# Transposing the attention weights in two half-height instructions instead of one

## The chip, the cores and the metric

The kernel runs on one core of a Trainium2 chip. The metric is the time of one launch in microseconds of device time, taken as the median of several runs; lower is better. PE is TensorE, with its weight loads shown apart as PEld; DVE is VectorE, ACT ScalarE, POOL GpSimd, SP the engine that issues the DMAs.

## The reference

Per batch and head (8 x 8 heads, 576 positions, 64 wide) two attentions are added: one over q, k and v averaged in groups of four (144 positions), repeated back to 576, and one local, in which a position sees those less than four away. The eight heads side by side are then x, the input of a mixture of four causal attentions, of which each position uses two.

```python
def _attn_ref(q, k, v):
    q_d = q.reshape(B, H, Sd, factor, D).mean(axis=3)      # k_d, v_d alike
    out_up = np.repeat(sm_attn(q_d, k_d, v_d), factor, axis=2)
    mask = np.abs(pos[:, None] - pos[None, :]) < factor
    ...
    return out_up + np.matmul(attn, v)

def _moe_ref(x, w_gate, wq, wk, wv, wo):
    logits = x @ w_gate                                     # the best 2 of 4, softmax over them: w
    for e in range(E):
        ...
        a = softmax(causal(scale * (x @ wq[e]) @ (x @ wk[e]).T))
        out += gate_e * (a @ (x @ wv[e]) @ wo[e])
```

## The kernel before

All sums are in fp32; the projections use float32r pairs (a high and a low part, three products each). The work on a batch has three stages. **Stage 1** (`s1_local`, `s1_down`, `s1_out`) goes through the four pairs of heads. Local scores are computed for ten tiles of 64 windows (`sc`), their softmax lies in `lp`; the pooled scores (`scd`) have 144 columns and lie in `dp`. In both, one head's rows lie on partitions 0 to 63 and the other's on 64 to 127. `s1_out` transposes them on TensorE (`tp`), copies them out of PSUM into `pt` and `pd`, and multiplies them with v into `o`, from which DVE builds x. **Stage 2** (`s2_q`, `s2_k`, `s2_v`, `s2_gate`) projects x; these are the dense products with 256 to 320 columns on the whole 128x128 array. **Stage 3** (`s2_scores`, `s2_trans`, `s2_av`, `s2_out`) works on two pairs of experts: scores `sq` of 64 rows of queries against all keys up to them, for two experts on the two halves of the partitions, softmax into `pr` buffers, transposes into `tq`, copies into `pta` and `ptb`, products with the values, and the output projection `po`. The stages of consecutive batches overlap: batch b is in stage 1 while b-1 is in stage 2 and b-2 in stage 3.

Products with a contraction of 64 run as 64x64 tiles, four of which lie on the array at once; in fp32 each is two hardware instructions, which is why the trace counts 40 for the 20 products of `local`.

A transpose is a TensorE instruction with the data as stationary operand and the identity as moving one. Before, it takes 128 partitions (122 or 112 where fewer are needed) by 128 columns, and one PSUM tile `tp` or `tq` holds both heads side by side. Where two blocks of rows stand the other way round on the partitions, `turned`, the identity with its halves exchanged, puts them right.

The order of the instructions is made by a planner in the kernel (`Plan`). Each operation is given its engines, an estimate of its length and its buffers; `ORDER` holds a priority for each, found ahead of time. `schedule` plays the engines forward and, on TensorE, prefers to stay in one kind of work (`MODE`, `SWX`, `SWM`) and puts in filler products on zeros (`wu`) when too little would run on the array. Copies out of PSUM may go to ACT or DVE (`"AV"`), subtractions and scalings to POOL or DVE. PSUM has two large buffers and four small ones of one bank; each transpose group before holds one small bank.

The pooling matrix `pool`, with which the first batch's v is averaged on TensorE (line 752), is built at the start by POOL: `count` writes indices, `fill_pool` turns them into a band of ones with comparisons and a product.

Of the kernel before, what the change touches and what calls it, by code (L numbers as in the profile page):

```python
# [1303 lines left out]
```

## Time and profile before

| | us |
|---|---|
| median of 3 runs | 494.53 (493.98 to 495.52) |
| the profiled execution | 495.67 |
| its span, first to last instruction | 493.9 |
| PE busy | 480.6 (97%) |
| DVE / ACT / POOL busy | 373.7 / 340.1 / 320.7 |
| mean granted clock of TensorE | 0.997 |

A row of the timeline merges equal instructions that follow each other on an engine. Its second number ends with the last one's recorded end, which for a product lies well after the next one's start, as products are pipelined. What an instruction costs the engine is therefore read from the distance between starts.

### The profile page before, as it was taken

Reading aid. Unit: us, or ns where it says so; the run is one execution under the profiler, and the core shown is the slowest. Engines: PE = TensorE matmul, PEld = TensorE weight load, DVE = VectorE, ACT = ScalarE, POOL = GpSimd, SP = SyncE. Lnnn points to the kernel's source line nnn. Section 1 sums busy time; section 2 is a strip of 40 time slices with the busy share of each in tenths; the row PEclk is TensorE's granted clock in tenths of the full one; section 3 lists DMA queues with packets and bytes.
Section 4 is the critical chain, followed back from the end, with each engine's and each line's share of the span. In section 5 each row is a group of like instructions: output and inputs, shape, how many; then the busy total and the mean of one; then the engine's idle time right before and its main releaser. Section 6 shows DMA issues by size and latency. Waiting matters only on the chain.

```text
span 493.9 us, 19034 instructions
## 1 busy us (share of the span) xinstructions
PE 480.6 (97%) x7691; PEld 431.1 (87%) x7693; DVE 373.7 (76%) x1163; ACT 340.1 (69%) x1110; POOL 320.7 (65%) x456
## 2 busy tenths in 40 slices
PE   7889999999999999999999999999999999999998
PEld 3769997999999898988999997999999887998886
DVE  8798998977868977688775888799596977342861
ACT  2697568768757758666877687757586776556773
...
PEclk9899999999999999999999999999999999999999
...
GB/s 201 242 242 108 179 157 161 121 66 69 155 100 109 184 37 119 107 159 52 71 200 75 72 115 102 148 114 109 30 237 62 45 1 3 49 32 30 49 51 97
DMA packets 43456, 52.62 MB, mean 107 GB/s; under 512 B 3304, under 2 KB 26344, under 8 KB 43368
## 3 DMA queue, kind: packets, MB, share of 16 engines
...
q8 instruction: 61, 1.00, 0.9%
...
## 4 chain that ended last, share of the span: by engine, by line
PE 79%; DVE 6%; ACT 6%; POOL 5%; DMA 3%; issue 2%; SPq 0%; POOLq 0%; DVEq 0%; ACTq 0%
PE pj L880 17%; PE po L1163 9%; PE pv L921 9%; PE sq L1025 8%; PE tq L1091 7%; PE o L1140 6%; PE o L839 4%; PE sc L694 3%; PE tp L821 3%; DMA lq<-in_qT_dram 3%; PE tp L810 3%; PE scd L767 2%; PE pv L752 2%; ACT pr L1046 1%; PE o L845 1%
## 5 line engine op out<-in xcount | busy, mean ns | idle before, releaser
L1054 POOL TENSOR_SCALAR pr<-pr,pst,gt 128x448 f32<-128x448 f32 (+8 forms) x89 | 67.0, 760 | 50.3 <-DVE pst L1051 41.4
L1046 ACT ACTIVATE pr<-pr,pst 128x320 f32<-128x320 f32 (+8 forms) x144 | 79.9, 556 | 21.6 <-DVE pst L1043 20.9
L880 PE MATMUL pj<-xh,wqk_h 128*128 128x320 f32 (+1 forms) x248 | 76.4, 308 | 0.0
L1043 DVE CUSTOM_DVE_ANT_0 pr<-sq,causal_t 128x192 f32<-128x192 f32 (+8 forms) x144 | 65.5, 483 | 11.4 <-PE sq L1025 10.8
L880 PE MATMUL pj<-xl,wqk_h 128*128 128x320 f32 (+1 forms) x248 | 72.9, 294 | 0.0
L880 PE MATMUL pj<-xh,wqk_l 128*128 128x320 f32 (+1 forms) x248 | 72.9, 294 | 0.0
L1025 PE MATMUL sq<-k,q 64*64 64x256 f32 (+6 forms) x768 | 56.1, 372 | 0.0
L1091 PE MATMUL tq<-ident,pr 128*128 128x128 f32 x368 | 51.8, 276 | 0.5 <-ACT ptb L511 0.3
L880 PEld LDWEIGHTS pj<-xh,wqk_h 128*128 128x128 f32 x248 | 46.6, 188 | 2.3 <-issue 0.8
L880 PEld LDWEIGHTS pj<-xh,wqk_l 128*128 128x128 f32 x248 | 46.7, 188 | 0.0
L880 PEld LDWEIGHTS pj<-xl,wqk_h 128*128 128x128 f32 x248 | 46.6, 188 | 0.0
L1091 PEld LDWEIGHTS tq<-ident,pr 128*128 128x128 f32 x368 | 41.0, 140 | 4.4 <-issue 1.2
L779 ACT ACTIVATE dp<-scd,dst 128x144 f32<-128x144 f32 x96 | 35.3, 379 | 13.7 <-DVE dst L774 13.1
L1152 POOL TENSOR_TENSOR ol<-oc,oh 128x256 fp32r<-128x256 f32 (+1 forms) x29 | 23.2, 803 | 32.0 <-ACT oh L1151 32.0
L715 POOL TENSOR_TENSOR lp<-lp,lst 128x640 f32<-128x640 f32 x27 | 34.6, 1280 | 13.0 <-DVE lst L714 11.3
L1025 PEld LDWEIGHTS sq<-k,q 64*64 64x64 f32 x768 | 32.5, 133 | 11.0 <-issue 1.4
L863 POOL TENSOR_TENSOR xl<-x,xh 128x576 fp32r<-128x576 f32 x25 | 35.6, 1424 | 3.9 <-ACT xh L862 3.8
L921 PE MATMUL pv<-wvg_h,xh 128*128 128x260 f32 x128 | 37.3, 292 | 0.0
L921 PE MATMUL pv<-wvg_h,xl 128*128 128x260 f32 x128 | 36.2, 283 | 0.0
L921 PE MATMUL pv<-wvg_l,xh 128*128 128x260 f32 x128 | 36.2, 283 | 0.0
L1163 PE MATMUL po<-oh,wo_h 128*128 128x256 f32 (+1 forms) x112 | 35.2, 314 | 0.0
L746 POOL TENSOR_TENSOR lr<-lr 128x512 f32<-128x512 f32 x27 | 34.7, 1285 | 0.0
...
## 6 DMA issues: line engine op xcount, KB each, us to landing
...
vx<-vg SPq DMA_DIRECT2D x8, 128.0 KB
```

The costliest lines, as they stand in the source:

```text
L715: op("l_nrm", "GV", (pool_tt(n), dve(n)), lambda e: eng[e].tensor_tensor(p(), p(), st[:, :, 2:3].to_broadcast([128, NT, W]), op=OP.mult), ...
L746: eng[e].tensor_tensor(vr[:, :, 0:2, :], vr[:, :, 0:2, :], vr[:, :, 2:4, :], op=OP.add)
L779: A.activation(p()[:, t, :], scs[t // 2]()[:, SD * (t % 2):SD * (t % 2) + SD], AF.Exp, bias=st[:, t, 4:5], scale=1.0 / 128.0, accum_out=st ...
L863: op("xl", "GV", (1360, dve(576)), lambda e: eng[e].tensor_tensor(xl(), x(), xh()[:, 0:S].bitcast(F32), op=OP.subtract), r=[x, (xh, 0)], w ...
L880: T.matmul(ps()[:, H0 + n0:H0 + n1], ww[:, c, w0 + 128 * p:w0 + 128 * p + 128], xx[b, c]()[:, n0:n1], start=(i == 0), stop=(i == 3 * NP - 1))
L921: T.matmul(ps()[:, :260], xx[b, c]()[:, 128 * t:128 * t + 128], ww[:, c, :], start=(i == 0), stop=(i == 3 * NP - 1))
L1025: T.matmul(pss[x]()[halves[e ^ (x % 2)], at + to:at + to + n1 - n0], q()[r, 64 * t:64 * t + 64], k()[r, n0:n1], start=True, stop=True)
L1043: op("s_max", "V", dve(n) + 4, lambda x=x, t=t, n=n, src=src: V.tensor_tensor_reduce(rows_of[t], src(), causal_t[:, S - 64:S + 256] if t = ...
L1046: op("s_exp", "A", 281 + n / 1.2, lambda x=x, t=t, n=n: A.activation(rows_of[t], rows_of[t], AF.Exp, bias=st[:, x, 4:5], scale=-1.0, accum ...
L1054: op("s_nrm", "GV", (327 + n / 1.2 + max(0, n - 384) * 1.1, 189 + n / 1.92), lambda g, x=x, t=t, n=n: eng[g].tensor_scalar(rows_of[t], row ...
L1091: T.transpose(ps()[:, 128 * x:128 * x + 128], block(t, j), turned if t % 2 else ident)
L1163: T.matmul(ps()[:, H1 + n0:H1 + n1], ww[:, p, 128 * c:128 * c + 128], xx[b, p]()[:, n0:n1], start=(i == 0), stop=(i == 5))
```

## The change

Every transpose becomes two instructions, one for each 64 partitions, with 64 columns of the identity, each into a PSUM bank of its own. A bank then holds one half of the partitions, for all blocks of the group, and the copies read one bank each; `pt`, `pd`, `pta` and `ptb` are laid out with the half ahead of the block. `turned` goes: the copy picks the half (`h ^ odd`). The groups of `s2_trans` become longer (up to seven blocks). The pooled scores' third tile is put on the same partitions as the others, since a transpose of one half must find one head there. The pooling matrix is built by DVE from the indices in two buffers, in two steps of three instructions. The planner's tables, estimates and the whole `ORDER` are new; `tp` and `trans` now count as the kind of work of the 64x64 products.

```diff
-XB, PTB = 1, 4
+XB, PTB = 1, 2
 ORDER = (
-    -402, -155, -134, -47, 246, 68, 331, 210, 256, -206, 122, 242, 359, 590, 448, 145, 425, 355, 456, 380, -84, 113,
...
-FR, TGT, TGT0, T0, TGT2, DW = -4.1, 3150.0, 3400.0, 228000.0, 3700.0, 12.6
+FR, TGT, TGT0, T0, TGT2, DW = -7.7, 3150.0, 3400.0, 450400.0, 3700.0, 16.5
...
-MODE = {"local": "quarter", ..., "scores": "quarter",
+MODE = {"local": "quarter", ..., "scores": "quarter", "tp": "quarter", "trans": "quarter",
...
+    def transpose(pss, z, data):
+        for x, r in enumerate(halves):
+            T.transpose(pss[x]()[:, z:z + 64], data[r, 0:128], ident[r, r])
...
 def count():
             for x, r in enumerate(halves):
-                G.iota(ck()[r, 0:640]...
+                for ck, z0, z1, k0 in ((cks[0], 0, 512, 0), (cks[1], 0, 128, 4)):
+                    G.iota(ck()[r, z0:z1]...
+        def above():
+            for x, n0, n1, own_x in ((0, 0, 512, 0), (1, 0, 128, 1), (1, 128, 192, 0)):
+                V.tensor_scalar(ges[x]()[:, n0:n1], cks[x]()[:, n0:n1], 0.0, own[:, own_x:own_x + 1], op0=OP.is_ge, op1=OP.mult)
         def fill_pool():
-            for x, n0, n1 in ((0, 0, 512), (1, 512, 640), (0, 640, 704)):
-                G.tensor_scalar(ge()[:, n0:n1], ck()[:, n0:n1], 0.0, own[:, x:x + 1], op0=OP.is_ge, op1=OP.mult)
-            G.tensor_scalar(lt(), ck(), 3.5, None, op0=OP.is_lt)
-            G.tensor_tensor(pool[:, 0:5, :]..., lt()[:, 0:640], ge()[:, 0:640], op=OP.mult)
+            for x, n0, n1 in ((0, 0, 512), (1, 512, 640)):
+                V.scalar_tensor_tensor(flat[:, n0:n1], cks[x]()[:, 0:n1 - n0], 3.5, ges[x]()[:, 0:n1 - n0], op0=OP.is_lt, op1=OP.mult)
...
-                    T.matmul(scs[t // 2]()[halves[h ^ (t // 2)], SD * (t % 2):SD * (t % 2) + SD],
+                    T.matmul(scs[t // 2]()[r, SD * (t % 2):SD * (t % 2) + SD],
...
-        for n0, n in ((0, 3), (3, 2)):
-            ps, pt = small("tp"), buf(wk, [128, n, 2, TQ], "pt", PTB)
-                for j in range(n):
-                    T.transpose(ps()[:, 128 * j:128 * j + rows], p()[0:rows, 2 * (n0 + j):2 * (n0 + j) + 2], ident[0:rows, 0:rows])
+        pss, pt = [small("tp") for _ in halves], buf(wk, [128, 2, 5, TQ], "pt", PTB)
+            for j in range(5):
+                transpose(pss, 64 * j, p()[:, 2 * j:2 * j + 2, :].rearrange("p t w -> p (t w)"))
+        for x in range(2):
+            op("tp_ev", "AV", (act(5 * TQ), dve(5 * TQ)), lambda e, x=x, pss=pss: copy(
+                e, pt()[:, x], pss[x]()[:, 0:320]...[:, :, 0:TQ]), r=[pss[x]], w=[(pt, x)])
...
-        jobs = {..., 3: [[(6, 0), (6, 1), (6, 2)], [(5, 0), (5, 1), (5, 2)]],
-                4: [[(8, 0), (8, 1), (8, 2)], [(8, 3), (8, "d")], [(7, 0), (7, 1), (7, 2), (7, 3)]]}[u]
+        jobs = {..., 3: [[(6, 0), (6, 1), (6, 2), (5, 0), (5, 1), (5, 2)]],
+                4: [[(8, 0), (8, 1), (8, 2), (8, 3), (8, "d")], [(7, 0), (7, 1), (7, 2), (7, 3)]]}[u]
...
-                    T.transpose(ps()[:, 128 * x:128 * x + 128], block(t, j), turned if t % 2 else ident)
+                    transpose(pss, 64 * x, block(t, j))
...
+            for h in range(2):
+                op("t_ev", "AV", (act(k) + m, dve(k) + m), lambda e, h=h, ev=ev: ev(e, h), r=[pss[h]],
```

Two places in the order on the engines. The first is TensorE at batch 0's first products of stage 3. `pr_131`, `pr_130` and the like are the softmax rows of one block of queries, `tq` and `tp` the transposes, `o` the products with v or with the values. Before:

```order
L880 MATMUL pj<-xl,wqk_h 128x256
L1091 MATMUL tq<-ident_121,pr_128 128x128 x2
L1091 MATMUL tq<-ident_121,pr_133 128x128 x2
L810 MATMUL tp<-ident_121,lp 128x122 x3
L1091 MATMUL tq<-ident_121,pr_131 128x128 x3
L1091 MATMUL tq<-ident_121,pr_130 128x128 x4
L1091 MATMUL tq<-ident_121,pr_133 128x128 x4
L1091 MATMUL tq<-ident_121,pr_129 128x128 x3
L1091 MATMUL tq<-ident_121,pr_131 128x128 x2
L810 MATMUL tp<-ident_121,lp 128x122 x2
```

and now:

```order
L879 MATMUL pj<-xl,wqk_h 128x256
L556 MATMUL tq<-ident,pr_130 128x64 x8
L838 MATMUL o_2198<-pt,lv 64x58 x12
L556 MATMUL tq<-ident,pr_131 128x64 x10
L838 MATMUL o_2198<-pt,lv 64x58 x4
L838 MATMUL o_2198<-pt,lv 64x56 x4
L1137 MATMUL o_2235<-pta,vg 64x192 x2
```

Four blocks of 128 columns have become eight instructions of 64, and the transposes that stood together in one run are strewn between 64x64 products: over the whole program TensorE goes from transposes to 64x64 products 79 times where it went 44 times, and back 64 times where it went 30 times; between dense and 64x64 products it goes 86 times (65 before), between dense products and transposes 88 times (79 before). It has 49 fillers where it had 37.

The second is the start, on POOL. `ck` are the indices, `dh`, `qd` and `kd` the averaged q and k, `lr` rings of rows of v. Before:

```order
L591 IOTA ck 64x640
L593 IOTA ck 64x64
L734 TENSOR_TENSOR dh<-lq 128x288
L735 TENSOR_TENSOR qd<-dh 128x144
L619 MEMSET lr_98 128x512
L614 MEMSET pool 128x256
L619 MEMSET lr_99 128x512
L598 TENSOR_SCALAR ge<-ck,own 128x512
L598 TENSOR_SCALAR ge<-ck,own 128x128
L598 TENSOR_SCALAR ge<-ck,own 128x64
L599 TENSOR_SCALAR lt<-ck 128x704
L600 TENSOR_TENSOR pool<-lt,ge 128x640
```

and now on DVE, where `lp` are the first local scores with their mask:

```order
L610 MEMSET causal_t 128x256
L611 MEMSET causal_t 128x128
L612 TENSOR_SCALAR causal_t<-nrow 128x64
...
L600 TENSOR_SCALAR ge<-ck,own 128x512
L600 TENSOR_SCALAR ge<-ck,own 128x128
L600 TENSOR_SCALAR ge<-ck,own 128x64
L703 SCALAR_TENSOR_TENSOR lp<-sc,lmask 128x640
L706 TENSOR_REDUCE lst_72<-lp 128x10
L605 SCALAR_TENSOR_TENSOR pool<-ck,ge 128x512
L605 SCALAR_TENSOR_TENSOR pool<-ck,ge 128x128
L607 SCALAR_TENSOR_TENSOR pool<-ck,ge 128x2x32
```

The five large passes have left POOL; on DVE there are six smaller ones, behind the masks and around the first local scores.

## Rows read from the trace of the kernel before

**Rows 1.** The page of the kernel before: busy time of each engine with its share of the span and its instructions, and the granted clock of TensorE in tenths of full speed in 40 equal slices of the span.

```profile
PE 480.6 (97%) x7691; PEld 431.1 (87%) x7693; DVE 373.7 (76%) x1163; ACT 340.1 (69%) x1110; POOL 320.7 (65%) x456
...
PEclk9899999999999999999999999999999999999999
```

**Rows 2.** The page: the chain of work that ended last, by engine.

```profile
PE 79%; DVE 6%; ACT 6%; POOL 5%; DMA 3%; issue 2%; SPq 0%; POOLq 0%; DVEq 0%; ACTq 0%
```

**Rows 3.** Groups of PE's instructions by line and shape: out<-in, shape, count | busy us, mean ns of one as recorded | idle before.

```profile
L1091 PE MATMUL tq<-ident,pr 128*128 128x128 f32 x368 | 51.8, 276 | 0.5 <-ACT ptb L511 0.3
...
L810 PE MATMUL tp<-ident,lp 122*128 122x122 f32 x160 | 24.8, 272 | 0.9 <-DVE lp L715 0.3 <-DVE pst L1043 0.3 <-ACT pt L511 0.2
...
L821 PE MATMUL tp<-ident,dp 112*128 112x112 f32 x96 | 19.4, 260 | 0.0
L821 PE MATMUL tp<-ident,dp 128*128 128x128 f32 x64 | 18.2, 290 | 3.2 <-ACT dp L788 0.8 <-ACT pta L511 0.7 <-ACT ptb L511 0.5
```

**Rows 4.** PE's timeline around 156 us, instructions that follow each other merged: start us, us from the first start to the last end, what, count.

```profile
155.82 0.28 PE L880 MATMUL pj<-xh,wqk_l 128*128 128x256 f32 x1
155.94 0.28 PE L880 MATMUL pj<-xl,wqk_h 128*128 128x256 f32 x1
156.06 0.93 PE L1091 MATMUL tq<-ident,pr 128*128 128x128 f32 x7
156.82 0.37 PE L821 MATMUL tp<-ident,dp 128*128 128x128 f32 x2
157.12 0.57 PE L839 MATMUL o<-pt,lv 64*64 64x58 f32 x24
157.52 0.55 PE L1025 MATMUL sq<-k,q 64*64 64x192 f32 x9
```

**Rows 5.** PE's timeline from 161 to 164 us, the same columns.

```profile
161.01 0.81 PE L694 MATMUL sc<-lk,lq 64*64 64x64 f32 x40
161.64 0.72 PE L1025 MATMUL sq<-k,q 64*64 64x64 f32 x12
162.29 0.74 PE L810 MATMUL tp<-ident,lp 122*128 122x122 f32 x5
162.96 0.81 PE L694 MATMUL sc<-lk,lq 64*64 64x64 f32 x40
163.70 0.41 PE L880 MATMUL pj<-xh,wqk_h 128*128 128x320 f32 x1
```

**Rows 6.** The timeline from 6 to 14 us, all engines, the rows that make or wait for the pooling matrix and one two-input pass of DVE; in brackets idle time before, and what ended it.

```profile
6.24 3.20 POOL L598 TENSOR_SCALAR ge<-ck,own 128x512 f32<-128x512 int32 x3
...
8.04 0.81 DVE L697 SCALAR_TENSOR_TENSOR lp<-sc,lmask 128x640 f32<-128x640 f32 x1
...
9.40 1.98 POOL L599 TENSOR_SCALAR lt<-ck 128x704 f32<-128x704 int32 x1
...
11.46 1.53 POOL L600 TENSOR_TENSOR pool<-lt,ge 128x640 f32<-128x640 f32 x1
...
13.05 1.30 PE L752 MATMUL pv<-lv,pool 128*128 128x128 f32 x7 [2.48 <-POOL pool L600]
```

**Rows 7.** Stretches of 25 us: length, then busy us (and instructions) of PE, PEld, DVE, ACT and POOL, the granted clock, DMA share and GB/s.

```profile
25.00:50.00 25.00, 23.01 (x458) 19.92 (x458) 22.37 (x63) 21.41 (x76) 21.61 (x22) 1.00 0.64 172
50.00:75.00 25.00, 24.47 (x454) 23.06 (x453) 22.63 (x64) 15.76 (x56) 21.89 (x27) 1.00 0.54 163
75.00:100.00 25.00, 23.82 (x422) 21.63 (x425) 22.27 (x64) 19.99 (x66) 22.77 (x30) 1.00 0.50 140
```

**Rows 8.** Weight loads in the timeline, from 171.9 and from 157.0 us: start us, us from the first start to the last end, what, count.

```profile
172.10 0.20 PEld L821 LDWEIGHTS tp<-ident,dp 128*128 128x128 f32 x2 [0.53 <-DVE oc L1149]
...
157.12 0.31 PEld L839 LDWEIGHTS o<-pt,lv 64*64 64x64 f32 x14 [0.16 <-issue]
```

**Rows 9.** Groups of weight loads (PEld) by line and shape, columns as in rows 3.

```profile
L839 PEld LDWEIGHTS o<-pt,lv 64*64 64x64 f32 x1280 | 28.4, 134 | 4.8 <-issue 2.7 <-DVE pst L1051 0.2 <-ACT pta L511 0.2
...
L821 PEld LDWEIGHTS tp<-ident,dp 128*128 128x128 f32 x64 | 8.9, 140 | 5.8 <-ACT pta L511 1.2 <-ACT dp L788 0.9 <-ACT ptb L511 0.8
```

**Rows 10.** PE's timeline from 176 to 177.2 us.

```profile
176.01 0.57 PE L839 MATMUL o<-pt,lv 64*64 64x58 f32 x24
176.51 0.66 PE L1091 MATMUL tq<-ident,pr 128*128 128x128 f32 x4
177.00 0.38 PE L810 MATMUL tp<-ident,lp 122*128 122x122 f32 x2
```

**Rows 11.** PE's timeline from 41.9 us, at the pooled scores.

```profile
41.92 0.56 PE L767 MATMUL scd<-kd,qd 64*64 64x144 f32 x10
42.27 0.34 PE L845 MATMUL o<-pd,vd 64*64 64x144 f32 x2
```

**Rows 12.** Groups of DVE's instructions by line and shape, columns as in rows 3.

```profile
L513 DVE COPY ptb<-tq 128x384 f32<-128x384 f32 x21 | 11.5, 552 | 15.5 <-PE tq L1091 15.5
...
L513 DVE COPY pd<-tp 128x192 f32<-128x192 f32 x17 | 5.9, 351 | 3.8 <-PE tp L821 3.6
```

**Rows 13.** Two stretches, 25 to 100 us and the rest, for the instructions that write or read tq alone, then for those of tp: length, then busy us (and instructions) of PE, PEld, DVE and ACT, the granted clock, DMA share and GB/s.

```profile
25.00:100.00 75.00, 3.13 (x23) 2.52 (x23) 0.98 (x2) 2.68 (x7) 1.00 0.56 159
...
25.00:100.00 75.00, 13.01 (x87) 9.38 (x85) 7.50 (x18) 6.50 (x18) 1.00 0.56 159
```

More of the change, by code (lines that the diff above doesn't have):

```diff
@@ L436 @@
 TICK = 10240 / 3
-MODE = {"local": "quarter", "down": "quarter", "o1": "quarter", "o1d": "quarter", "av": "quarter", "scores": "quarter",
+MODE = {"local": "quarter", "down": "quarter", "o1": "quarter", "o1d": "quarter", "av": "quarter", "scores": "quarter", "tp": "quarter", "trans": "quarter",
         "q": "dense", "k": "dense", "v": "dense", "wo": "dense"}
@@ L441 @@
        ("column", "quarter"): 100.0, ("quarter", None): 165.0, ("quarter", "dense"): 170.0, ("quarter", "column"): 150.0}
-LAG = {"scores": 85.0, "down": 60.0, "local": 50.0, "o1d": 20.0}
-SWM = {None: 1.3, "quarter": 1.1, "column": 1.8, "dense": 1.6}
+LAG = {"scores": 85.0, "down": 60.0, "local": 50.0, "o1d": 20.0, "tp": 40.0, "trans": 40.0}
+SWM = {None: 5.1, "quarter": 1.6, "column": 4.1, "dense": 4.9}
 SWB, MARG = 0, 2.0
-LOCK = {"V": {"vd", "xl", "l_sub", "l_nrm", "d_nrm", "xt", "wlo", "s_nrm", "o_lo"},
+LOCK = {"V": {"vd", "xl", "l_sub", "l_nrm", "d_nrm", "xt", "wlo", "s_nrm", "o_lo", "c_ge", "c_pool"},
         "G": {"vd", "kd", "qd", "l_sub", "l_nrm", "d_nrm", "xl", "xt", "wlo", "o_lo", "g_rank", "g_mask", "g_nrm"}}
-RATE = {"local": 2.1, "down": 1.2, "tp": 1.18, "trans": 1.18, "o1": 2.1, "o1d": 2.2, "av": 2.0, "scores": 2.1}
+RATE = {"local": 2.1, "down": 1.2, "tp": 2.1, "trans": 2.1, "o1": 2.1, "o1d": 2.2, "av": 2.0, "scores": 2.1}
 F32R_COL, F32R_MM = 0.4167, 13.2
+QT = 15.8
 def dense(n, cols):
@@ L604, in masks @@
+            z = [t()[:, 128:192].rearrange("p (k m) -> p k m", m=2 * WT) for t in (cks[1], ges[1])]
+            V.scalar_tensor_tensor(pool[:, 5:7, 64 - WT:64 + WT], z[0], 3.5, z[1], op0=OP.is_lt, op1=OP.mult)
         def masks():
@@ L614, in constants @@
         op("c_zero", "G", 320, lambda: G.memset(pool[:, 5:7, :], 0.0), w=[(PL, 1)])
-        op("c_cnt", "G", 1800, count, w=[ck], alloc=[ck])
-        op("c_pool", "G", 4100, fill_pool, r=[ck], w=[ge, lt, (PL, 1)], alloc=[ge, lt])
+        op("c_cnt", "G", 2100, count, w=cks, alloc=cks)
+        op("c_ge", "V", 560, above, r=cks, w=ges, alloc=ges)
+        op("c_pool", "V", 930, fill_pool, r=cks + ges, w=[(PL, 1)])
         plan.unit = ("constants", 1)
@@ L620, in constants @@
         plan.unit = ("constants", 2)
-        op("c_mask", "V", 650, masks, w=[CT])
-        op("c_rank", "V", 260, ranks, w=[ML])
+        op("c_mask", "V", 1370, masks, w=[CT])
+        op("c_rank", "V", 180, ranks, w=[ML])
     wqk_h = cst.tile([128, NP, 512], F32R, name="wqk_h")
@@ L815, in s1_out @@
-        pss, pd = [small("tp") for _ in range(2)], buf(wk, [128, 5, 2, NQD], "pd", NPD)
-        def trd(x):
-            flat, kr = dp().rearrange("p t w -> p (t w)"), 64 + NQD
-            jobs = (((2 * SD + WT, 208, 128), (SD + WT, 112, kr), (0, 0, kr)), ((2 * SD - 48, 112, 128), (SD - 64, 0, kr)))[x]
-            for at, z, n in jobs:
-                T.transpose(pss[x]()[:, z:z + n], flat[0:n, at:at + 128], turned if n == 128 else ident[0:n, 0:n])
-        def evd(e, x):
-            n = (3, 2)[x]
-            copy(e, pd()[:, 3 * x:3 * x + n], strided(pss[x]()[:, 0:NQD], (112 + 16 * x, n), (64, 2)))
@@ new lines, in s1_out, with trd @@
+        op("tp", "T", 20 * QT, tr, r=[p], w=pss, alloc=pss + [pt])
+        for x in range(2):
+            op("tp_ev", "AV", (act(5 * TQ), dve(5 * TQ)), lambda e, x=x, pss=pss: copy(
+                e, pt()[:, x], pss[x]()[:, 0:320].rearrange("p (j q) -> p j q", q=64)[:, :, 0:TQ]), r=[pss[x]], w=[(pt, x)])
+        pss, pd = [small("tp") for _ in halves], buf(wk, [128, 2, 5, NQD], "pd", NPD)
+        def trd(pss=pss):
+            flat = dp().rearrange("p t w -> p (t w)")
+            for i, at in enumerate((0, SD + WT, 2 * SD + WT, SD - 64, 2 * SD - 48)):
+                transpose(pss, 80 * i - 16 * (i in (2, 4)), flat[:, at:at + 128])
@@ L829, in s1_out @@
+        op("tp", "T", 20 * QT, trd, r=[dp], w=pss, alloc=pss + [pd])
+        for x in range(2):
+            op("tp_ev", "AV", (act(5 * NQD), dve(5 * NQD)), lambda e, x=x, pss=pss: copy(
+                e, pd()[:, x], pss[x]()[:, 0:400].rearrange("p (j q) -> p j q", q=80)[:, :, 0:NQD]), r=[pss[x]], w=[(pd, x)])
         o, up = big("o1"), buf(wk, [128, SD], "up")
@@ L831, in s1_out, with av @@
         xl = XL[b, c] = buf(wk, [128, S], "xl", 8, F32R)
-        def av(k0, pt):
-            for t in range(k0, k0 + pt.shape[1]):
+        def av(k0, k1):
+            for t in range(k0, k1):
                 z, n = TQ * t, min(TQ, SH - TQ * t)
@@ L1005, in s2_gate @@
         op("g_nrm", "G", 200, norm, r=[WR, gst], w=[cmt])
[L1006 removed]
+        op("g_out", "A", 1020, spread, r=[cmt], w=[gt], alloc=[gt])
     PT = {}
@@ L1081, in s2_trans @@
         for js in jobs:
-            ps, first = small("tq"), []
+            pss, first = [small("tq") for _ in halves], []
             parts = sorted(set(place(*x)[0] for x in js))
@@ L1099, in s2_trans @@
                 part, jj, q0 = place(t, j)
-                if runs and runs[-1][0] == part and runs[-1][4] != 2 and jj == runs[-1][2] + runs[-1][1] and q0 == runs[-1][3]:
-                    runs[-1][1] += 1
-                    runs[-1][4] = 1
-                elif runs and runs[-1][0] == part and runs[-1][4] != 1 and jj == runs[-1][2] and q0 == runs[-1][3] + 64 * runs[-1][1]:
-                    runs[-1][1] += 1
-                    runs[-1][4] = 2
-                else:
-                    runs.append([part, 1, jj, q0, 0, x])
@@ L1109, in ev @@
-            def ev(eng, runs=runs, ps=ps):
-                for part, n, jj, q0, way, x in runs:
-                    pt, src = PT[b, p, part], ps()[:, 128 * x:128 * (x + n)]
+                last = runs[-1] if runs else None
+                if last and last[0] == part and last[6] == t % 2 and last[4] != 2 and jj == last[2] + last[1] and q0 == last[3]:
+                    last[1] += 1
+                    last[4] = 1
+                elif last and last[0] == part and last[6] == t % 2 and last[4] != 1 and jj == last[2] and q0 == last[3] + 128 * last[1]:
+                    last[1] += 1
+                    last[4] = 2
+                else:
+                    runs.append([part, 1, jj, q0, 0, x, t % 2])
@@ L1112, in ev @@
+            def ev(eng, h, runs=runs, pss=pss):
+                for part, n, jj, q0, way, x, odd in runs:
+                    pt, src = PT[b, p, part], pss[h]()[:, 64 * x:64 * (x + n)].rearrange("p (j q) -> p j q", q=64)
                     if way == 2:
-                        copy(eng, pt()[:, jj, :, q0:q0 + 64 * n].rearrange("p e (t q) -> p t e q", q=64),
-                             src.rearrange("p (t e q) -> p t e q", e=2, q=64))
-                    else:
-                        copy(eng, pt()[:, jj:jj + n, :, q0:q0 + 64], src.rearrange("p (j e q) -> p j e q", e=2, q=64))
@@ L1117, in s2_trans @@
-            k, m = 128 * len(js), 60 * (len(runs) - 1)
-            op("t_ev", "AV", (act(k) + m, dve(k) + m), ev, r=[ps],
-               w=[(PT[b, p, x[0]], (x[0], x[2], x[3])) for x in runs])
+                        copy(eng, pt()[:, h ^ odd, jj, q0:q0 + 128 * n].rearrange("p (t q) -> p t q", q=128)[:, :, 0:64], src)
+                    else:
+                        copy(eng, pt()[:, h ^ odd, jj:jj + n, q0:q0 + 64], src)
+            k, m = 64 * len(js), 60 * (len(runs) - 1)
+            for h in range(2):
+                op("t_ev", "AV", (act(k) + m, dve(k) + m), lambda e, h=h, ev=ev: ev(e, h), r=[pss[h]],
+                   w=[(PT[b, p, x[0]], (x[0], x[2], x[3], h ^ x[6])) for x in runs])
@@ L1140, in mm @@
                         T.matmul(obs[x]()[r, q0:q1], vg()[kr, j, 64 * (2 * p + e):64 * (2 * p + e) + 64],
-                                 pt()[kr, j, e, q0:q1], start=j == 0, stop=j == len(jobs) - 1 and part == 0 and x == 1)
+                                 pt()[kr, e, j, q0:q1], start=j == 0, stop=j == len(jobs) - 1 and part == 0 and x == 1)
             for x, jj, q0, to, vv, at in tails:
@@ L1144, in mm @@
                     T.matmul(obs[x]()[r, to:to + 64], vv()[halves[x], at, 64 * (2 * p + e):64 * (2 * p + e) + 64],
-                             pt()[halves[x], jj, e, q0:q0 + 64], start=to < z, stop=(x, at) != (1, 1))
+                             pt()[halves[x], e, jj, q0:q0 + 64], start=to < z, stop=(x, at) != (1, 1))
         cost = 15 + 1.667 * (sum(q1 - q0 for _, q0, q1 in jobs) + 64 * (len(tails) + 1) // 2) + 8 * (len(jobs) + 1)
```

63 lines of the change are left out of this document (23 added, 40 removed), and 278 rows, old and new, of the table ORDER.

## The prediction

> **What bounds the kernel now.** I read the page first. PE is busy 97% of the span, DVE 76%, ACT 69%, POOL 65%, and the granted clock stands at nine tenths or more of full speed (2.4 GHz) in every slice but the second [rows 1]. The chain that ended last is PE for 79% of the span [rows 2]. Because a busy PE is not a PE at its peak, I then went to the timeline and priced PE by the distance between starts, not by the recorded duration. Seven transposes of 128 columns reach from 156.06 to 156.82, 0.109 us each, though one is recorded with 0.276 us [rows 3, 4]. Five of 122 columns take 0.67 with a head and a tail that I price below, so 0.104 each [rows 5]. Priced so, dense products, 64x64 products, transposes, the pooling product and the fillers add up to some 433 us of the 494: PE is the bound nearly throughout, and a microsecond of PE work saved is close to a microsecond of time. The exceptions are the start, where PE sits idle 2.48 us for the pooling matrix [rows 6], and the stage from 25 to 100 us, where DVE is busy 22.4, 22.6 and 22.3 us of each 25 [rows 7].
>
> **The transposes.** Removed: 368 of 128 columns (0.109 each, 40.1 us), 160 of 122 (0.104, 16.6), and 64 of 128 and 96 of 112 columns on line 821 (7.0, and at 0.095 in proportion to the columns 9.1): 72.8 us of PE [rows 3 to 5]. Added: 2 x 688 instructions of 64 partitions and 64 columns. No row shows such a pair. The nearest is a round of four 64x64 instructions on the same array: 40 of them take 0.63 [rows 5], less the first uncovered load of 0.057 that is 0.0144 each, 0.058 for a round of four with 64 columns. The 58-column ones give the same (24 in 0.40) [rows 4], so the round is set by its loads as much as by its columns. A new pair moves 64 columns in each half, as a round does, and loads two blocks of 64x128, as many weights as a round's four blocks of 64x64. So I take 0.058. From below it is 64 columns at the old pace, 0.0545. From above it is two loads one behind the other: a load of 128 columns keeps the next one off for 0.06 (two take 0.20, one lasts 0.140) [rows 8, 9], 0.114 for the pair. Sum: 688 x 0.058 = 39.9, **a gain of 32.9 us**, with bounds of 35.3 gained and 5.6 lost.
>
> **Changes of tile shape.** From dense products to 128x128 transposes nothing is lost: 155.94 to 156.06 is the pace of the dense ones. From transposes into 64x64 work it costs 0.094 (156.82 to 157.12 is 0.30, of which the two transposes are 0.206) [rows 4]. Out of 64x64 work it costs 0.11 for the drain (40 take 0.74 before a dense product, 0.63 before more 64x64 work; 24 take 0.50 before a transpose, 0.40 otherwise) and 0.056 for the first load that nothing covers [rows 4, 5, 10], 0.166 together. In the order of both programs I count the borders. Before: 70 into 64x64 work, 69 out of it, 18.0 us. After, if the new 64x128 instructions mix freely with 64x64 ones, as the 64x64 ones mix among themselves: 88 in and 86 out, 22.6 us, **4.5 lost**. If they drain against 64x64 work as well, 79 more into it and 64 more out of it: 40.6 us, 22.6 lost. If they mix with the dense ones instead, 11.5 lost; if with both, 6.6 won. No row decides, since the kernel before has no 64x128 instruction. I take the first, because what mixes with 64x64 work in the trace also uses the halves of the rows apart; both ends stay in the range. The Trainium skill speaks against this (TensorEngine Tiling, Key Properties): it says that a change of tiling mode, other than a change of tile, drains the engine, and it lists 64x128 and 64x64 as different configurations. The trace has the drain, 0.11 us, but only between 128x128 and 64x64. By that rule it is the second of the four sums above.
>
> **The scores of the pooled stage (line 767).** The third pair of products now writes the same two quarters of the array as the first two. Before, the third's passes ran beside them: ten passes take 0.35 [rows 11], 0.035 each where two quarters alone would give 0.06. At worst two passes of 0.12 come on top in each of 32 units, 7.7 us; at best the next 64x64 work fills the free quarters. I take **2 us lost**, nearer to the best because 64x64 work follows at once in these rows.
>
> **The copies out of PSUM.** The same columns leave PSUM in more and smaller copies: DVE gets 193 where it had 112, ACT 219 where it had 160. A DVE copy of 384 columns takes 0.552, one of 192 0.351 [rows 12]: about 0.15 fixed and 1.05 ns per column. Worked out over the forms, DVE gets some 18 us more. With the other work that the new order shifts to and from DVE (three more poolings of each kind, four fewer subtractions) DVE goes from 374 to about 392 us, 83% of a span of 474. Between 25 and 100 us, where 110 of the 688 transposes stand [rows 13], a sixth, it would reach 70.6 us of 75, so that this stage can hardly shrink: 5 of its 5.8 us are not won. Elsewhere DVE goes from 73% to about 82%; its answers come later, and the new order has twelve more fillers, all of them in its first sixth, which marks where PE has to be kept busy; I put 4 us on that. **9 us lost**, from 2 to 16. What hides the copies now is the PE work between a transpose and its user; were that cover gone, PE would wait for a copy of 0.35 to 0.45 per group. Each group now takes two of the four small PSUM banks, at nothing, since the groups per pair of heads fall from seven or eight to five.
>
> **The pooling matrix.** The large passes on POOL reach from 6.24 to 12.99 us [rows 6]. DVE has no such rows; its nearest is 0.81 for 640 columns, so two passes over 704 columns are about 1.8, behind the index counting that stays on POOL. PE's idle time of 2.48 goes, except what DVE's own queue (the masks and the first local scores stand ahead) takes back: **2 us gained**, from 0 to 2.5. Table entries alone move instructions, and cost nothing by themselves.
>
> **Sum.** -32.9 + 4.5 + 2 + 9 - 2 = -19.4. The profiled execution took 495.67 us, a span of 493.9 and 1.8 around it; that gives 476.3. It lies 1.1 above the median of the runs, so the forecast is 475.
>
> **The rivals.**
> 1. The new transposes drain against 64x64 work. For it: every border between shapes that the trace has costs 0.1 to 0.17. Against it: they share the halves of rows. 18 us more, of which the waits give back 4, since a slower PE waits less: 489.
> 2. They mix with dense work and not with 64x64 work: 7 more at the borders, 482. For it: both use all 128 columns of the array. Against it: one uses whole rows, the other halves.
> 3. The loads of the two halves do not overlap, and the change ends **slower**: 0.114 a pair, 688 x 0.114 = 78.4 for 72.8, 5.6 lost where 32.9 were to be gained. With the borders (4.5), the pooled scores (2), waits of 2 on a PE that is slower, and the start (-2) it is 12 on top: 507. It decides from about 0.086 a pair, where the gain is used up. Against it: fourteen 64-column loads go in 0.31 [rows 8], a round of four in 0.06 where each is recorded with 0.134 [rows 9], so loads into different parts do overlap. By the Trainium skill (TensorE: Matmul & The Clock Gate, LDWEIGHTS) a load takes its columns over 1.2 per ns, whatever the rows, so 107 ns for 128 columns, and a pair could not be shorter than that. The trace disagrees: the second load of 128 columns began 0.06 after the first [rows 8].
> 4. The new transposes drain against nothing and DVE follows: 6.6 gained at the borders in place of 4.5 lost, waits of 4: 459. DVE's share in the stage from 25 to 100 us speaks against it [rows 7].
> 5. It does not do what it says: the halves overlap in part (0.08 to 0.09 a pair), and the extra borders take the rest: 493 to 496.
>
> **Chances.** The forecast 0.54 (467 to 482); rival 1 0.17 (483 to 492.5); rival 2 0.09; rival 3 0.10; rival 4 0.05; rival 5 0.05. A measurement of this kernel tells 0.3%, 1.5 us, from no change. Faster: 0.54 + 0.17 + 0.09 + 0.05, less 0.01 for the slow end of rival 1: 0.84. Same: 0.05. Slower: 0.11. The range runs from 463 to 492, which leaves out rivals 3 and 5 and most of 4.
>
> **What would show it.** In the profile after, eight new transposes in a row should take 0.23 to 0.25 us from the first start to the next group's; 0.45 is rival 3. A row of 64x64 work ahead of a transpose should take no longer than ahead of more 64x64 work; 0.11 longer is rival 1. The lines of the pooling matrix should leave POOL, and the first pooling product start near 11 us. DVE should be busy near 390 us. A granted clock under full speed anywhere after the start would make all of it wrong, since every price here was read at full speed.

## The result, and the profile after

The kernel after takes 501.33 us (median of 4 runs, 500.68 to 502.54) where the kernel before, on the same chip, took 495.02 (4 runs, 493.98 to 495.68). The ratio is 1.0132, with a 95% interval of 1.0104 to 1.0161: slower by 1.3%, where 475 had been forecast. The profiled execution took 501.08 us, 5.4 more than the one of before, with a span of 499.3.

The page of the kernel after: busy time, the granted clock, the chain by engine [rows 1, 2].

```profile
PE 487.9 (98%) x8391; PEld 423.7 (85%) x8393; DVE 392.2 (79%) x1256; ACT 334.8 (67%) x1150; POOL 314.7 (63%) x451
...
PEclk9989999999999999999999999999999999999999
...
PE 83%; DVE 10%; ACT 3%; DMA 2%; issue 1%; POOL 1%; SPq 0%; DVEq 0%; ACTq 0%; POOLq 0%
```

PE bounds it more than before, at the same clock. DVE's 392.2 us are the 392 of the prediction. So the loss must be looked for on PE. The groups of PE by shape [rows 3]:

```profile
L556 PE MATMUL tq<-ident,pr 64*128 64x64 f32 x736 | 38.5, 232 | 2.1 <-ACT oh L1148 0.7 <-DVE oc L1146 0.5 <-DVE ptb L511 0.4
...
L556 PE MATMUL tp<-ident,dp 64*128 64x64 f32 x320 | 17.5, 232 | 1.2 <-DVE vd L511 0.8 <-ACT dp L794 0.2 <-DVE pt L511 0.2
L556 PE MATMUL tp<-ident,lp 64*128 64x64 f32 x320 | 16.8, 231 | 0.3 <-DVE pst L1042 0.3
```

The recorded busy time fell from 114 us to 73, and says nothing of the price. PE's timeline from 294.6 us, where all four kinds of border stand within 2 us, does [rows 4, 5]:

```profile
294.52 0.28 PE L929 MATMUL pv<-wvg_h,xh 128*128 128x260 f32 x1
294.63 0.28 PE L929 MATMUL pv<-wvg_l,xh 128*128 128x260 f32 x1
294.84 0.52 PE L556 MATMUL tp<-ident,lp 64*128 64x64 f32 x10
295.30 0.81 PE L700 MATMUL sc<-lk,lq 64*64 64x64 f32 x40
296.04 0.53 PE L556 MATMUL tp<-ident,dp 64*128 64x64 f32 x10
296.49 0.38 PE L1160 MATMUL po<-oh,wo_h 128*128 128x256 f32 x1
```

Read it by starts. Dense products follow each other by 0.12, but the first transpose comes 0.21 after the last of them: for 0.09 PE starts nothing. This is the drain, and there is none in [rows 4]. Ten half transposes, five pairs, take 0.46 and 0.45. The trace has a pair every 0.061 within a run, so five are 0.31; 0.05 goes for the first pair's load, which nothing covers (the second pair starts 0.112 after the first), and 0.10 for a drain at the end, towards 64x64 work and dense work alike. The 40 products of the local scores take 0.74 ahead of transposes, where they took 0.63 ahead of other 64x64 work [rows 5]: 0.11 again. Drain and first load together are some 0.15 for each border. **The 64x128 instructions drain against both other shapes, on both sides.** The whole trace has it so, not these two microseconds alone: the last pair of a run stands 0.156 us from what follows, ahead of 64x64 work (76 runs) as ahead of dense work (38), where another pair would stand at 0.062 (medians without waits, worked out from the starts). Behind it the second dense product comes 0.225 after the first, where 0.12 is their pace, so the border into dense work costs some 0.20; out of the old transposes it cost 0.03.

For the whole kernel I added up, by the tile written, the time from each matmul's start to the next one's, its slot (worked out from the traces; waits and drains lie with the instruction ahead of them; the last three columns are experiments below):

| us | before | after | third_other | more_borders | quarter_products |
|---|---|---|---|---|---|
| transposes (tq, tp) | 83.9 | 67.2 | 68.5 | 115.8 | 111.0 |
| dense (pj, pv, po) | 218.7 | 225.4 | 226.3 | 225.5 | 225.5 |
| pooled scores (scd) | 15.1 | 26.2 | 20.0 | 25.8 | 26.2 |
| o, sq, sc | 151.8 | 155.8 | 155.4 | 155.3 | 159.7 |
| fillers, pooling product | 22.1 | 22.1 | 22.2 | 24.0 | 22.2 |
| sum | 491.4 | 496.7 | 492.3 | 546.3 | 544.6 |

(The 115.8 contain the added one-column products, 144 x 0.204 = 29.4. Such sums agree with the spans within rounding and the two ends.) The change won 16.7 us on the transposes' own slots, not 32.9, and gave back 6.7 on dense work, 4.0 on 64x64 work and 11.1 on the pooled scores.

The copies on DVE, the largest groups [rows 12], and the stage that the prediction took for the tightest [rows 7]:

```profile
L511 DVE COPY pt<-tp 128x290 f32<-128x290 f32 x35 | 15.1, 451 | 4.9 <-PE tp L556 4.8
L511 DVE COPY ptb<-tq 128x192 f32<-128x192 f32 x38 | 11.8, 351 | 7.0 <-PE tq L556 6.9
```

```profile
25.00:50.00 25.00, 22.80 (x422) 19.52 (x421) 23.48 (x64) 19.86 (x67) 21.68 (x21) 0.93 0.66 193
50.00:75.00 25.00, 25.00 (x481) 22.94 (x480) 18.67 (x55) 17.25 (x58) 20.84 (x25) 1.00 0.46 123
75.00:100.00 25.00, 24.43 (x468) 20.90 (x468) 23.43 (x74) 20.66 (x79) 22.84 (x33) 1.00 0.49 140
```

DVE has 65.6 us here, not the 70.6 that were worked out, and PE 72.2. The start, DVE's and PE's timeline [rows 6]:

```profile
8.46 1.96 DVE L605 SCALAR_TENSOR_TENSOR pool<-ck,ge 128x512 f32<-128x512 int32 x2
```

```profile
10.05 1.83 PE L758 MATMUL pv<-lv,pool 128*128 128x128 f32 x14
12.36 0.81 PE L700 MATMUL sc<-lk,lq 64*64 64x64 f32 x40 [0.49 <-DMA lq<-in_qT_dram]
```

The matrix left POOL, and the first pooling product starts at 10.05 without a wait, where it started at 13.05 after 2.48 of idle time.

### The profile page after: what moved, and what is told of

It is laid out like the page before. It is cut to its first block, busy times and chain, and to the rows that moved or that the text cites. A ratio compares the mean times of both kernels' runs of the same rounds, so it can differ in the third digit from the quotient of the medians.

```text
span 499.3 us, 20630 instructions
## 1 busy us (share of the span) xinstructions
PE 487.9 (98%) x8391; PEld 423.7 (85%) x8393; DVE 392.2 (79%) x1256; ACT 334.8 (67%) x1150; POOL 314.7 (63%) x451
## 4 chain that ended last, share of the span: by engine, by line
PE 83%; DVE 10%; ACT 3%; DMA 2%; issue 1%; POOL 1%; SPq 0%; DVEq 0%; ACTq 0%; POOLq 0%
PE pj L879 21%; PE po L1160 9%; PE pv L920 9%; PE sq L1024 8%; PE o L1137 6%; PE tq L556 6%; PE tp L556 5%; PE o L838 4%; PE scd L773 4%; PE sc L700 3%; PE o L844 2%; PE pv L929 1%; DVE pr L1042 1%; PE po L1184 1%; DMA wst<-in_wo_dram 1%
## 5 line engine op out<-in xcount | busy, mean ns | idle before, releaser
L1045 ACT ACTIVATE pr<-pr,pst 128x192 f32<-128x192 f32 (+8 forms) x144 | 80.0, 558 | 26.6 <-DVE pst L1042 24.6
L1053 POOL TENSOR_SCALAR pr<-pr,pst,gt 128x192 f32<-128x192 f32 (+8 forms) x88 | 58.7, 671 | 56.7 <-DVE pst L1050 39.6
L879 PE MATMUL pj<-xh,wqk_h 128*128 128x320 f32 (+1 forms) x248 | 77.8, 314 | 0.0
L1024 PE MATMUL sq<-k,q 64*64 64x256 f32 (+6 forms) x768 | 57.3, 374 | 0.2 <-DVE x L856 0.2
L862 POOL TENSOR_TENSOR xl<-x,xh 128x576 fp32r<-128x576 f32 x29 | 41.3, 1426 | 9.2 <-ACT xh L861 9.2
L785 ACT ACTIVATE dp<-scd,dst 128x144 f32<-128x144 f32 x96 | 35.2, 374 | 10.8 <-DVE dst L780 10.3
L556 PE MATMUL tq<-ident,pr 64*128 64x64 f32 x736 | 38.5, 232 | 2.1 <-ACT oh L1148 0.7
L511 DVE COPY ptb<-tq 128x192 f32<-128x192 f32 (+4 forms) x95 | 29.7, 348 | 12.6 <-PE tq L556 12.2
L556 PEld LDWEIGHTS tq<-ident,pr 64*128 64x128 f32 x736 | 29.1, 138 | 11.6 <-issue 3.5
L752 POOL TENSOR_TENSOR lr<-lr 128x512 f32<-128x512 f32 x28 | 36.3, 1296 | 0.0
```

What stands on the lines that cost most here:

```text
L556: T.transpose(pss[x]()[:, z:z + 64], data[r, 0:128], ident[r, r])
L752: eng[e].tensor_tensor(vr[:, :, 0:2, :], vr[:, :, 0:2, :], vr[:, :, 2:4, :], op=OP.add)
L785: A.activation(p()[:, t, :], scs[t // 2]()[:, SD * (t % 2):SD * (t % 2) + SD], AF.Exp, bias=st[:, t, 4:5], scale=1.0 / 128.0, accum_out=st ...
L862: op("xl", "GV", (1360, dve(576)), lambda e: eng[e].tensor_tensor(xl(), x(), xh()[:, 0:S].bitcast(F32), op=OP.subtract), r=[x, (xh, 0)], w ...
L879: T.matmul(ps()[:, H0 + n0:H0 + n1], ww[:, c, w0 + 128 * p:w0 + 128 * p + 128], xx[b, c]()[:, n0:n1], start=(i == 0), stop=(i == 3 * NP - 1))
L1024: T.matmul(pss[x]()[halves[e ^ (x % 2)], at + to:at + to + n1 - n0], q()[r, 64 * t:64 * t + 64], k()[r, n0:n1], start=True, stop=True)
```

## The experiments

Three explanations are tested. Theory A: the drains of the new shape took what the transposes won. Theory B: the third pair of pooled scores, now behind the first two, costs several times the 2 us of the prediction. Theory C, the rival: PE's work did shrink, and more copies on DVE took it back.

**third_other** (after):

```diff
-                    T.matmul(scs[t // 2]()[r, SD * (t % 2):SD * (t % 2) + SD],
+                    T.matmul(scs[t // 2]()[halves[h ^ (t // 2)], SD * (t % 2):SD * (t % 2) + SD],
```

> The kernel after, with only the third pair of products of the pooled scores put back on the two quarters of the array that the first two pairs leave free (the third tile then holds the two heads' rows the other way round, and what reads it is not changed, so the outputs of the pooled part mix two heads). Theory B, that the third pair now runs behind the first two instead of beside them: the slots of this line fall from 26.2 us to about 15, the time from 501.3 to 490 to 493. The prediction's own size of this term (2 us): 499. Theory A (borders between tile shapes) and theory C (DVE is late) say nothing of it, and by C alone, PE not being the bound, the time would stay within 1 us.

Measured: 495.60 us, ratio to before 0.9999 (0.9979 to 1.0019), 6 us less than after.

**before_third_same** (before):

```diff
-                    T.matmul(scs[t // 2]()[halves[h ^ (t // 2)], SD * (t % 2):SD * (t % 2) + SD],
+                    T.matmul(scs[t // 2]()[r, SD * (t % 2):SD * (t % 2) + SD],
```

> The kernel before, with only the third pair of products of the pooled scores put on the same two quarters as the first two (the third tile's heads change places, as in the other run, and what reads it is not changed). Theory B: 8 to 11 us slower, 503 to 506 beside 495. The prediction's size: 497. If the free quarters are filled by the next 64x64 work: under 1 us.

Measured: 500.96 us, ratio 1.0120 (1.0083 to 1.0157), 5.4 us more. Both ways the line costs 5 to 6.5 us: nearly three times the prediction's 2, less than the 8 to 11 I expected of theory B. The groups of PE by shape in after, third_other, before and before_third_same, in this order:

```profile
L773 PE MATMUL scd<-kd,qd 64*64 64x144 f32 x384 | 31.1, 290 | 0.0
```

```profile
L773 PE MATMUL scd<-kd,qd 64*64 64x144 f32 x384 | 22.7, 294 | 0.0
```

```profile
L767 PE MATMUL scd<-kd,qd 64*64 64x144 f32 x384 | 22.4, 294 | 0.5 <-DVE kd L732 0.5
```

```profile
L767 PE MATMUL scd<-kd,qd 64*64 64x144 f32 x384 | 30.6, 288 | 0.4 <-DVE kd L732 0.4
```

The mean of one doesn't move (288 to 294 ns); what moves is how much of it lies beside another. The timelines of after and of third_other at the same work:

```profile
60.44 0.82 PE L773 MATMUL scd<-kd,qd 64*64 64x144 f32 x9
60.99 0.26 PE L838 MATMUL o<-pt,lv 64*64 64x58 f32 x1
```

```profile
60.86 0.58 PE L773 MATMUL scd<-kd,qd 64*64 64x144 f32 x10
61.18 0.30 PE L838 MATMUL o<-pt,lv 64*64 64x58 f32 x4
```

The next 64x64 work starts 0.55 after the first pooled product in the one and 0.32 in the other: it doesn't fill the free quarters. 32 units by 0.23 are 7.4; the rest of the 11.1 us that the slots of scd gained is the new order's. That it is held up because it stands behind the third pair in PE's queue is argued from the order, not shown: in third_other four passes start within 0.03 us, where after has two and then none for 0.17. So the third pair starts there ahead of the second, and PE does let some work pass.

**less_dve** (after):

```diff
-  ... V.tensor_reduce(st[:, :, 0], p(), op=OP.add, axis=AX.X) ...
+  ... V.tensor_reduce(st[:, :, 0], p()[:, :, 0:32], op=OP.add, axis=AX.X) ...
...
-  V.tensor_reduce(dst()[:, 0:n], s4, op=OP.add, axis=AX.X)
+  V.tensor_reduce(dst()[:, 0:n], s4[:, :, 0:2], op=OP.add, axis=AX.X)
```

> The kernel after, with less work on DVE and nothing else changed: the sums of the local probabilities read 32 of the 64 columns of each tile, and DVE's poolings of q and k read two of the four columns (both leave out half of a sum, so the numbers differ). DVE's busy time falls by some 22 us, from 392 to about 370, below what it was in the kernel before (374). Theory A and B, that the loss is PE work: 0 to 3 us faster, 498 to 501. Theory C, that the more and smaller copies on DVE hold PE up: 10 us or more faster, 491 or less.

Measured: 500.27 us, ratio 1.0095 (1.0069 to 1.0121), 1 to 2 us less than after. The page:

```profile
PE 487.9 (98%) x8393; PEld 424.0 (85%) x8393; DVE 372.3 (75%) x1256; ACT 334.4 (67%) x1150; POOL 314.8 (63%) x451
```

20 us less on DVE, and PE's busy time to the tenth the same. Nor did PE wait more than before: span less busy time is 11.4 us in after, 13.3 in before. Theory C falls.

**more_borders** (after), once in each group of transposes:

```diff
...
+  T.matmul(pss[0]()[lo, 511:512], ident[lo, 0:64], ident[lo, 0:1], start=True, stop=True)
```

> The kernel after, with a 64x64 product of one column added in the middle of each of the 144 groups of half transposes, on the lower half's quarter and into a column of PSUM that nobody reads. Theory A, that 64x128 transposes and 64x64 products drain against each other on both sides: 0.136 + 0.166 = 0.30 us for each group, 43 us in all, of which waits may give back some: 530 to 545. The prediction's assumption that the two mix freely: two passes of 0.015 to 0.03 each, 4 to 9 us, 505 to 510. Theory C: less than 5 us, since PE would have slack.

Measured: 549.82 us, ratio 1.1110 (1.1072 to 1.1148), 48.5 us more than after: 0.337 for each of the 144, a little over the 0.30 of theory A, with nothing given back. Counted without idle time and at full clock, PE's work grew by 46.9 us, 0.33 each. PE's timeline at the work that was shown of after:

```profile
321.82 0.28 PE L937 MATMUL pv<-wvg_l,xh 128*128 128x260 f32 x1
322.03 0.34 PE L560 MATMUL tp<-ident,lp 64*128 64x64 f32 x4
322.30 0.27 PE L555 MATMUL tp<-ident 64*64 64x1 f32 x2
322.50 0.40 PE L560 MATMUL tp<-ident,lp 64*128 64x64 f32 x6
322.83 0.81 PE L704 MATMUL sc<-lk,lq 64*64 64x64 f32 x40
```

The two passes of one column keep the next transpose off for 0.20, and the five pairs reach over 0.80 in place of 0.46.

**quarter_products** (after):

```diff
-  T.transpose(pss[x]()[:, z:z + 64], data[r, 0:128], ident[r, r])
+  for c, rc in enumerate(halves):
+      T.matmul(pss[x]()[rc, z:z + 64], data[r, 64 * c:64 * c + 64], ident[r, r], start=True, stop=True)
```

> The kernel after, in the same order, with each half transpose replaced by two 64x64 products with the identity, so that this work has the tile shape of the other 64x64 work. Each block is then 8 passes of 64 columns in place of 2: two rounds of four at 0.058 us, 0.117 for 0.061, 38 us more. Theory A: the 143 borders between transposes and 64x64 work vanish with it, 79 x 0.136 + 64 x 0.166 = 21 us, so 517 to 520. If these borders cost nothing: 538 to 541.

Measured: 547.11 us, ratio 1.1006 (1.0966 to 1.1046), above both. The timeline and the waits of PE:

```profile
321.13 0.28 PE L930 MATMUL pv<-wvg_l,xh 128*128 128x260 f32 x1
321.34 0.81 PE L557 MATMUL tp<-ident,lp 64*64 64x64 f32 x40
321.97 0.76 PE L701 MATMUL sc<-lk,lq 64*64 64x64 f32 x40
322.55 0.94 PE L557 MATMUL tp<-ident,dp 64*64 64x64 f32 x40
323.43 0.39 PE L1161 MATMUL po<-oh,wo_h 128*128 128x256 f32 x1
```

```profile
PE tq L557 <- issue: 7.7, 6, 1.9
PE tp L557 <- issue: 5.3, 5, 2.3
PE o L839 <- issue: 3.0, 2, 2.1
PE o L1142 <- issue: 3.0, 3, 1.2
PE sq L1025 <- issue: 1.4, 1, 1.4
```

The borders did vanish: the 40 products of the local scores take 0.58, not 0.74, and the first five blocks 0.63, 0.17 more than in after, where the passes alone add 0.28. The whole trace says the same by its medians: five blocks of `tp` between dense products take 0.741 where they took 0.456 in after, all of the 0.28; ahead of 64x64 work, 0.631 for 0.456; between 64x64 work, 0.588 for 0.456. (The second five blocks of this row, 0.88, are slower than the others of their kind, 0.80; they hold pauses of up to 0.05.)

But PE sits idle 20.4 us in these five rows, 22.8 in all 20 waits of this kind, put down to "issue" (in after all such waits are 1.0 us). Without them it would be some 524, nearer to theory A's 517 to 520 than to 538. The queue that loads instructions, after and then quarter_products, tells what they are:

```profile
q8 instruction: 66, 1.08, 0.9%
```

```profile
q8 instruction: 98, 1.61, 1.3%
```

Its packets have 16 KB, and there is one for every 254 to 256 products and weight loads of PE in both kernels: it is PE's own program. Counted in PE's records, the 20 waits lie whole multiples of 256 apart, to within one, and each ends 1.2 to 1.8 us after a packet has landed (worked out from the trace). So PE waited for instructions. Why these packets came too late and others didn't is open, so the run supports theory A by its rows more than by its time.

**third_fixed** (after): third_other with the third tile's heads put right.

```diff
...
-  for i, at in enumerate((0, SD + WT, 2 * SD + WT, SD - 64, 2 * SD - 48)):
+  for i, at in enumerate((SD - 64, 0, SD + WT, 2 * SD + WT, 2 * SD - 48)):
...
-  e, pd()[:, x], pss[x]()[:, 0:400].rearrange("p (j q) -> p j q", q=80)[:, :, 0:NQD]) ...
+  e, pd()[:, x ^ z, a:n], pss[x]()[:, 80 * a:80 * n].rearrange("p (j q) -> p j q", q=80)[:, :, 0:NQD])
+  for z, a, n in ((0, 0, 3), (1, 3, 5)) ...
...
```

> The kernel after with the third pair of the pooled scores on the other two quarters, as in the first of these runs, and the third tile's heads now put right in the copies out of PSUM: its blocks stand last in each bank and are copied to the other half's place, two copies for one (64 copies more over ACT and DVE, some 0.15 us each). Theory B by the runs so far (5.5 us for this line): 495 to 497. If the additional copies held PE up: 499 or more, but less work on DVE brought 1.1 us only, so they should cost under 1.

Measured: 498.05 us, ratio 1.0044 (1.0009 to 1.0080): 3 to 4.5 us less than after, and still no faster than before. That is above the 495 to 497 expected. After and the profiled execution of this kernel (499.45) each have one wait of PE, at local scores some 24 us into the span, for which the profile names nothing ("issue"):

```profile
PE sc L700 <- issue: 0.8, 1, 0.8
```

```profile
PE sc L700 <- issue: 3.3, 1, 3.3
```

They stand at the same place, the 704th and the 706th of PE's records, and are of the kind that quarter_products explains: in this execution a late load of instructions accounts for 2.5 us.

**fewer_borders** and **far_fewer_borders** (third_fixed, the planner's table; 24.0 for 6.0 in the second):

```diff
...
-  "tp": "quarter", "trans": "quarter"
+  "tp": "row", "trans": "row"
...
+  ("dense", "row"): 146.0, ("row", "dense"): 151.0, ("quarter", "row"): 150.0, ("row", "quarter"): 140.0
...
-  SWM = {None: 5.1, "quarter": 1.6, "column": 4.1, "dense": 4.9}
+  SWM = {None: 5.1, "quarter": 6.0, "row": 6.0, "dense": 6.0}
-  FR, TGT, TGT0, T0, TGT2, DW = -7.7, 3150.0, 3400.0, 450400.0, 3700.0, 16.5
+  FR, TGT, TGT0, T0, TGT2, DW = -7.7, 2100.0, 2100.0, 450400.0, 3700.0, 16.5
...
```

> The kernel of third_fixed, with the planner told that the half transposes are a kind of their own that drains against both others (0.14 to 0.17 us at each change of kind, where it had put them with the 64x64 products), a patience of 6 for all kinds, and a lower mark for fillers. The order that comes out has 290 changes of kind where after has 337 (tr and 64x64: 98 for 143), and 42 fillers for 49. Theory A: 47 borders at 0.15 and 7 fillers at 0.43, 7 + 3 us less than third_fixed: 485 to 489, if the new order makes no new waits; a table of due times that was made for another order speaks for some, so up to 495. If the borders cost nothing: 493 to 496, from the fillers alone.

> As fewer_borders with a patience of 24: 258 changes of kind, 58 fillers. Theory A: 79 borders at 0.15 less, 11.8 us, 9 fillers more, 3.9 us: 486 to 490, plus the waits that a patience of 24 makes, which may take all of it back (up to 500).

Measured: 532.47 us (1.0739, 1.0680 to 1.0797) and 549.62 (1.1078, 1.1016 to 1.1141). Both miss, by 35 us and more. The page of fewer_borders:

```profile
PE 497.8 (94%) x8386; PEld 422.9 (80%) x8386; DVE 381.9 (72%) x1269; ACT 345.4 (65%) x1210; POOL 315.6 (59%) x453
...
PE   6987998999999899999799998999899999999998
...
PEclk9699999999999988999879997999999999999999
```

PE is idle 32.9 of 530.7 us, against 14.2 of 497.7 in third_fixed, and the clock is granted at 0.965 on the mean, against 0.993: the slices at 0.7 or 0.8 of full speed (15th, 16th, 20th, 21st and 25th; a part of each at 1.2 GHz, the rest at 2.4) hold idle time of PE or stand behind a slice that does (the 14th, 20th and 25th, one to three tenths idle). Others as idle, the 4th, 7th and 29th, keep full speed. 18.7 us of idle time and some 15 of clock are all of the 33 by which the spans differ, and leave nothing for the 7 us of the 47 borders. Both terms are too rough to rule these 7 out, and the last pair of a run stands 0.156 from what follows here too. These two runs tell that an order is worth more than the borders in it; they say nothing for theory A.

**matrix_on_pool** (after); the comparison in `above` goes to POOL in the same way:

```diff
-  V.scalar_tensor_tensor(flat[:, n0:n1], cks[x]()[:, 0:n1 - n0], 3.5, ges[x]()[:, 0:n1 - n0], op0=OP.is_lt, op1=OP.mult)
+  G.tensor_scalar(lt, cks[x]()[:, 0:n1 - n0], 3.5, None, op0=OP.is_lt)
+  G.tensor_tensor(flat[:, n0:n1], lt, ges[x]()[:, 0:n1 - n0], op=OP.mult)
...
```

> The kernel after, with the pooling matrix built by POOL instead of DVE, in the same order. The prediction's price of this part is 2 us (0 to 2.5); the two traces show the third local scores begin at 12.36 us in after and at 15.78 in before. So 2 to 3.5 us slower than after, 503 to 505; if DVE's queue or the first stage takes it back anyway, within 1 us of 501.3.

Measured: 505.55 us, ratio 1.0192 (1.0140 to 1.0244), 3 to 4 us more than after. PE's timeline has the wait back:

```profile
13.74 2.57 PE L762 MATMUL pv<-lv,pool 128*128 128x128 f32 x12 [3.75 <-POOL pool L607]
```

**before_matrix_dve** (before), the version that the others point to:

```diff
-  G.tensor_scalar(ge()[:, n0:n1], ck()[:, n0:n1], 0.0, own[:, x:x + 1], op0=OP.is_ge, op1=OP.mult)
+  V.tensor_scalar(ge()[:, n0:n1], ck()[:, n0:n1], 0.0, own[:, x:x + 1], op0=OP.is_ge, op1=OP.mult)
...
-  G.tensor_scalar(lt(), ck(), 3.5, None, op0=OP.is_lt)
-  G.tensor_tensor(pool[:, 0:5, :].rearrange("p k m -> p (k m)"), lt()[:, 0:640], ge()[:, 0:640], op=OP.mult)
+  V.scalar_tensor_tensor(pool[:, 0:5, :].rearrange("p k m -> p (k m)"), ck()[:, 0:640], 3.5, ge()[:, 0:640], op0=OP.is_lt, op1=OP.mult)
...
```

> The kernel before, in the same order on PE, with its pooling matrix built by DVE in three steps (compare, then compare and multiply) behind the index counting that stays on POOL. The one part of the change that gained: put back on POOL it cost 3 us (1.0192 for 1.0132). PE's idle time of 2.48 us ahead of the first pooling product should go: 2 to 3 us faster than before, 492 to 493.5, and the fastest of all these kernels. If DVE's own queue holds the matrix up as long: within 1 us of before.

Measured: 494.74 us beside 496.40, ratio 0.9969 (0.9948 to 0.9991), the lowest of all. PE's timeline:

```profile
9.72 1.72 PE L751 MATMUL pv<-lv,pool 128*128 128x128 f32 x14
12.88 0.81 PE L693 MATMUL sc<-lk,lq 64*64 64x64 f32 x40 [1.44 <-DMA lk<-in_kT_dram]
```

The pooling product comes 3.3 us earlier and, with 1.44 of waiting for k, the next local scores 2.9 earlier (12.88, where before has 15.78). Of that some 1.5 us is left at the end. Further on PE waits 2.1 us in all for `dp` from ACT, where before waits 0.8; the rest was not traced.

## Why the prediction was wrong

- **The pair's price was right.** 0.061 us measured, 0.058 forecast; 688 x 0.061 = 42 for 72.8, a gain of 30.8 where 32.9 stood. Rival 3 (loads one behind the other, 0.114) falls: the loads of two halves start 3 ns apart.
- **The failed step is the change of tile shape.** Four sums were worked out from the borders, and the prediction took the one in which 64x128 mixes freely with 64x64 (4.5 us lost), because both use the halves of the rows apart. It drains against 64x64 and dense work: that is the second sum, 22.6. Its price into 64x64 work was too low as well: 0.094, the drain alone, where drain and first load are 0.15; 79 x 0.056 = 4.4 more, 27 in all. The Trainium skill (TensorEngine Tiling, Key Properties and Available Configurations) had been quoted for this: a change of tiling mode drains, and 64x128 and 64x64 are two modes. The trace after agrees, with 0.09 to 0.11 us of drain at each border. Rival 1 named this mechanism, with a chance of 0.17. more_borders shows the price by itself, and quarter_products shows it gone when the shape is that of the neighbours.
- **Part of it is the order.** The table was made as if the new transposes were of one kind with the 64x64 work, so the order has 337 changes of shape where the kernel before had 236 (143 for 74 between transposes and 64x64 work). That a better order exists for the new shape is argued, not shown: the two that were tried lost far more in waits.
- **The pooled scores were mis-sized**, 2 us where the runs show 5 to 6.5, near the 7.7 that the prediction had for the worst case. The row that I leaned on showed 64x64 work following at once; with the third pair on the same quarters it comes 0.23 later.
- **The copies**: DVE's 392 us came as forecast, but 20 us less on DVE bring only 1 to 2. The stage from 25 to 100 us was not the tight one. (The 5.8 us at stake there were too many: by the prediction's own prices 110 blocks by 0.048 are 5.3.)
- **The pooling matrix**: 3 to 4 us by matrix_on_pool in the new order, 1.5 in the old one; 2 had been forecast.
- **The sum again**: -30.8 + 27 + 6 - 3 is -0.8; the profiled execution is at +5.4. The slots without idle time and at full clock (worked out from the traces) show where the 6.2 lie. Transposes, dense and 64x64 work together are 5.5 us shorter, near the -3.8 of pairs and borders. The pooled scores are 10.3 longer; third_other still has 3.0 of them, which are the new order's and not the third pair's. The fillers are 2.8 longer, which the table's row hides, since in before it holds the wait for the pooling matrix. PE's idle time is 2.0 shorter. No run took the fillers out alone, so their part rests on the slots. The prediction had put 9 us on waits for copies; what came is work on PE. The time lies nearest to rival 3's 507, and by chance: its mechanism is not there.
